# Four chunks on one token block instead of two chunks on two blocks: a fast-multiplication MLP on one core

## The chip, the core and the metric

The kernel runs on one core of a Trainium2 chip. The engines named here are PE (TensorE, matrix products into PSUM), DVE (VectorE), ACT (ScalarE), POOL (GpSimd) and SP (SyncE, whose queue issues nearly all DMAs). The metric is the device time of one execution in microseconds; the runs shown are compared by their median. All arithmetic is float32 at the interface. Inside, a float32 operand is split into a rounded part ("hi", type float32r) and the remainder ("lo"), and a product is made of three passes: hi x hi, hi x lo and lo x hi.

## What is computed

A transformer block with adaptive layer norm over S = 2048 tokens of width D = 576, with an MLP of hidden width F = 4608. Cut to what matters:

```python
mod = (silu(c) @ w_mod).reshape(c.shape[0], 6, 1, -1)
sa, ca, ga, sb, cb, gb = (mod[:, i] for i in range(6))
h = layernorm(x) * (1 + ca) + sa
x = x + ga * linear_attention(h, A_wqkv, A_wo)      # 32 heads of 18, phi(t) = where(t>0, t+1, exp(t)) + 1e-6
h = layernorm(x) * (1 + cb) + sb
x = x + gb * (silu(h @ B_w1) @ B_w2)                # 576 -> 4608 -> 576
```

## The kernel before

Tokens are handled in 16 tiles of 128 and 4 blocks of 512. The hidden width is handled in 18 groups of 256 (two chunks of 128, `G2 = 2`, `NG = 18`). The work has three stages.

**Stage A** (to about 213 us of the profiled span): the modulation, the projections to k, v and part of q, and the sums over tokens of the linear attention. The change leaves it as it is, except that the temporary `e` of `phi` (L348) is handed in by the caller.

**Stage B** (213 to 398 us): the loop `while s < NT + 5 or filler or turns` (L798). Step s normalises the attention numerator of tile s, transposes tile s-1 and projects tile s-2 (`attn_out`, L572). Once the four tiles of a block are done, the block is normalised again and "turned" (`turn_all`, L702): transposed to the layout [feature, token], modulated, split to hi and lo, and the sums of its pieces that the fast multiplication needs are formed, split and stored to DRAM (`store_h`, L683). The first MLP group (g = 0) is done in this stage plainly: `load_mlp(0)` (L582) loads and splits its weights, and `mlp_units` (L659) puts six pieces of work a block on a list called `filler`: two `mlp_up` (14 matmuls of 512 columns each) and four `mlp_down` (12 matmuls of 288 columns each). `unit()` takes the next piece off the list, `turn_chunk()` the next piece of a turn. The order of the instructions on each engine in this stage is chosen by the framework's planner from the program's order and its own estimate of the times.

**Stage C** (398 us to the end) does the other 17 groups by a fast multiplication with seven products in place of eight (Strassen-Winograd). A unit is one group and one pair of blocks (`units`, L1106), so 34 units. In the up direction the 2x2 split is over the two blocks of the pair, the two 256-wide halves of the first 512 features, and the two chunks of the group; the last 64 features come in two additional matmuls in four of the seven products. One up product (`passes`, L949) is 6 or 8 matmuls of 128x128 weights on 512 tokens. `Unit.up(n)` (L970) then gathers products in three PSUM banks: product 1 is copied out, product 2 is added to 1, and 6, 5, 7, 4, 3 are read by DVE between accumulations into the same bank, so that the four results f (two blocks by two chunks) appear, to which ACT applies SiLU. Order of products: (1, 6, 2, 5, 7, 3, 4).

In the down direction the split is over two halves of 256 tokens of one block, the two chunks, and the two halves of the 576 output columns; each block of the pair has its own seven products (`down`, L1040), each of 12 / 2 = 6 matmuls of 288 columns, followed by one DVE addition of the PSUM bank into `acc` or `U` (L1054). `operands1` and `operands2` (L1015, L1023) form the token-side sums on POOL and split them (cast on ACT, difference on DVE or POOL). Within a unit, PE's order is written by hand: two down products of the unit before stand around each up product.

```python
if before:
    before.down(2 * q)
unit.up(n)
if before:
    before.down(2 * q + 1)
```

Of the 14 up operands of the two pairs, 10 are streamed from DRAM for each group (`STREAM`, L679; `fetch`, L933) into three rooms, and 4 stay in SBUF. `Weights` (L866) loads a group's weights (w1 and w2), forms their seven sums on POOL and splits each (cast on ACT, difference on DVE, `sub_hi`, L61); w1 is prepared during the unit before the group's first, w2 during the group's first. Only PE has a hand-written order in this stage (`manual_schedule(engines={PE})`, L1093); the others follow the planner. The last block of the last group goes down plainly (`plain_down`, L1079), with each tile stored as it is done.

## Time and profile before

Three runs took 1216.33, 1218.12 and 1222.57 us, with a median of 1218.12. The profiled execution took 1217.73 us.

| what | value |
|---|---|
| time of the profiled execution | 1217.73 us |
| its span, first to last instruction | 1215.7 us |
| first up product of stage C starts | 397.84 us |
| last up product of stage C, its last matmul starts | about 1194.7 us |
| PE busy over the span | 1158.4 us, 95% |
| DVE busy over the span | 984.3 us, 81% |
| POOL, ACT busy over the span | 599.8 us, 518.2 us |
| granted TensorE clock, mean | 0.993 |
| HBM read, written | 250.56 MB, 16.78 MB |

How to read it: the span is the time from the first to the last instruction that the profiler recorded. An engine's busy time is the union of its instructions. Matmuls overlap in PE's pipeline, so one matmul's listed duration is longer than the step to the next one, and a busy PE need not be a PE at its highest rate. In a group of instructions, the line of the source, the engine, the operation and the tiles (result, then inputs) come first, then the count; behind the bar stand the busy time in us and the mean duration of one in ns, then the idle time of the engine ahead of them with what ended it. In a list of waits, the numbers are the total in us, how often, and the longest. In a timeline a row has the start in us, the time to the end of the row's last instruction, and how many were merged; an idle time ahead of it stands in brackets. In rows by stretch, each engine has its busy time and, in brackets, its number of instructions; the last columns are the granted clock, the DMA engines' mean busy share and GB/s. In the view of one line, the three numbers behind the count are the shortest, the median and the longest duration in ns.

### The profile page before, as it was taken

The page shows a single profiled execution, that of the slowest core. Times are in us where ns is not written, and L with a number is a line of the kernel's source. Part 1 is how long each engine was busy: PE and PEld are TensorE (multiplying, and loading weights), DVE is VectorE, ACT ScalarE, POOL GpSimd, SP SyncE. Part 2 cuts the span into 40 slices and gives each one's busy share as a digit, 9 for nine tenths or more (in the row PEclk, how much of TensorE's full clock was granted, in tenths as well). Part 3 has the DMA queues.
Part 4 walks back from the last instruction along what each step waited for, and adds up shares of the span by engine and source line. Part 5 has one row for each costly group of instructions (what it writes and reads, how often), then busy time and mean ns, then how long its engine had stood idle before and what let it go on. Part 6 is the DMA issues. An engine that isn't in the chain of part 4 may idle for free. (4 is left out here: it accounts for less than half of the span.)

```text
span 1215.7 us, 19355 instructions
## 1 busy us (share of the span) xinstructions
PE 1158.4 (95%) x7167; PEld 1048.1 (86%) x7167; DVE 984.3 (81%) x1591; ACT 518.2 (43%) x1057; POOL 599.8 (49%) x676
## 2 busy tenths in 40 slices
PE   5999999999998799999999999999999999999997
PEld 4999999899988688888888889888888888888896
DVE  6746754888866688888898898888888888888887
ACT  4434342315545444444444444444444444444441
POOL 3200000332400665775676577577657747766772
PEclk9999999999998999999999999999999999999999
DMA  9213300213247778868769779769678687697664
GB/s 289 82 40 88 113 1 1 70 41 128 101 181 286 277 250 297 308 239 326 271 248 340 257 252 336 260 247 340 247 283 310 235 333 272 243 344 260 242 253 147
DMA packets 57580, 268.60 MB, mean 221 GB/s; under 512 B 5450, under 2 KB 20046, under 8 KB 34446
## 3 DMA queue, kind: packets, MB, share of 16 engines
q1 hardware_dynamic: 57486, 267.36, 61.2%
q8 instruction: 57, 0.93, 0.3%
q14 instruction: 37, 0.30, 0.1%
HBM read 250.56 MB, written 16.78 MB: 220 GB/s over the span
## 5 line engine op out<-in xcount | busy, mean ns | idle before, releaser
L1054 DVE TENSOR_TENSOR acc<-down,acc 128x576 f32<-128x576 f32 x335 | 245.7, 748 | 22.2 <-PE down L1050 17.1
L962 PE MATMUL up<-hT,w 128*128 128x512 f32 x876 | 225.9, 393 | 2.1 <-DMA hT<-hd 2.1
L962 PEld LDWEIGHTS up<-hT,w 128*128 128x128 f32 x876 | 156.2, 188 | 28.2 <-DMA hT<-hd 1.6
L1026 POOL TENSOR_TENSOR s<-f,f 128x256 f32<-128x256 f32 x67 | 52.7, 786 | 251.1 <-ACT f L1001 251.1
L1050 PEld LDWEIGHTS down<-w,hb 128*128 128x128 f32 x804 | 112.7, 188 | 35.2 <-DVE U L1054 11.5
L1050 PE MATMUL down<-w,hb 128*128 128x288 f32 x804 | 127.2, 300 | 15.0 <-DVE U L1054 13.6
L1054 DVE TENSOR_TENSOR U<-down,U 128x576 f32<-128x576 f32 x134 | 100.7, 752 | 48.6 <-PE down L1050 47.6
L154 PE MATMUL psK<-w,hT 128*128 128x288 f32 (+2 forms) x896 | 127.8, 301 | 2.5 <-DVE e L129 1.1
L154 PEld LDWEIGHTS psK<-w,hT 128*128 128x128 f32 x896 | 122.7, 192 | 4.4 <-DVE hT L62 2.1
L1050 PE MATMUL down<-w,hc 128*128 128x288 f32 x804 | 122.7, 295 | 0.3 <-DVE acc L1054 0.2
L1050 PEld LDWEIGHTS down<-w,hc 128*128 128x128 f32 x804 | 115.4, 188 | 7.0 <-DVE acc L1054 1.4
L1011 POOL TENSOR_TENSOR hc<-s,hc 128x512 fp32r<-128x512 f32 x67 | 94.4, 1409 | 12.0 <-ACT hc L1010 12.0
L1010 ACT CAST hc<-s 128x512 fp32r<-128x512 f32 x67 | 41.6, 621 | 117.1 <-POOL s L1028 117.0
L62 DVE TENSOR_TENSOR w<-raw,w 128x288 fp32r<-128x288 f32 (+2 forms) x139 | 83.3, 609 | 7.4 <-ACT w L903 7.0
L1001 ACT ACTIVATE f<-f 128x512 f32<-128x512 f32 x102 | 64.3, 630 | 55.1 <-DVE f L1000 55.1
L962 PE MATMUL up<-room,w 128*128 128x512 f32 x330 | 85.6, 394 | 1.3 <-DVE f L986 0.9
L1050 PE MATMUL down<-w,hd 128*128 128x288 f32 x402 | 65.2, 297 | 5.0 <-DVE acc L1054 5.0
L962 PEld LDWEIGHTS up<-room,w 128*128 128x128 f32 x330 | 58.8, 188 | 11.5 <-DVE f L986 1.4
L1050 PEld LDWEIGHTS down<-w,hd 128*128 128x128 f32 x402 | 57.5, 188 | 11.4 <-ACT f L1001 6.3
L154 PE MATMUL big<-w,qT 128*128 128x288 f32 x448 | 65.8, 300 | 0.8 <-DVE qT L62 0.7
L1028 POOL TENSOR_TENSOR s<-s,f 128x256 f32<-128x256 f32 x67 | 64.6, 964 | 2.7
L962 PE MATMUL up<-hT,wt 128*128 128x512 f32 x206 | 64.9, 396 | 0.0
(228 smaller groups left out, 2367.5 us busy)
## 6 DMA issues: line engine op xcount, KB each, us to landing
hT<-hd SPq DMA_DIRECT2D x69, 1280.0 KB, 5.5
hT<-hd SPq DMA_DIRECT2D x43, 1024.0 KB, 5.7
room<-hd SPq DMA_DIRECT2D x32, 1280.0 KB, 5.8
room<-hd SPq DMA_DIRECT2D x23, 1024.0 KB, 5.7
raw<-in_B_w_dram SPq DMA_DIRECT2D x18, 576.0 KB
raw<-in_B_w_dram SPq DMA_DIRECT2D x18, 512.0 KB, 6.8
hd<-S SPq DMA_DIRECT2D x6, 1024.0 KB
xt<-in_A_x_dram SPq DMA_DIRECT2D x16, 288.0 KB, 4.0
```

The source lines that it names most:

```text
L62: return V.tensor_sub(lo, full, f32(hi))
L154: T.matmul(ps, xpart(a), wpart(b), start=n == 0, stop=n == len(XW) - 1)
L962: T.matmul(ps, left, right, start=first and m == 0, stop=m == len(seq) - 1, skip_group_check=True)
L1001: A.activation(f, f, AF.Silu)
L1010: A.copy(t[:, :, 0, :], src)
L1011: eng.tensor_sub(t[:, :, 1, :], src, f32(t[:, :, 0, :]))
L1026: G.tensor_add(s[:, 0:1], half(i, 0, 1), half(i, 1, 1))
L1028: G.tensor_sub(s[:, 1:2], s[:, 0:1], half(i, 0, 0))
L1050: T.matmul(ps[:, p, :HALF], self.a[i, n][:, u, p * P : (p + 1) * P], self.w.w2[n][:, v], start=n in (1, 5, 7, 6) and j == 0, stop=j == 2, ...
L1054: V.tensor_add(dst, ps[:, :, :HALF], dst)
```

## The change

Groups 0 and 1 are both done plainly in stage B; the other 16 groups are taken two at a time ("double groups" d = 1 to 8, 512 hidden features, four chunks). A unit of stage C is now one double group and one block of 512 tokens: 8 x 4 = 32 units. In the up direction the token split is over the block's two halves of 256 tokens (`HT`), and each of the seven products is made twice, for the two subgroups s = 0 and 1, side by side in one PSUM bank. So an up product is 12 or 16 matmuls of 256 columns. In the down direction each product accumulates both subgroups in one bank: 12 matmuls of 288 columns and then one DVE addition. There are seven down products a unit and PE's order has one behind each up product. The order of products becomes (1, 6, 2, 5, 7, 4, 3).

All seven up operands of every block go to DRAM and are streamed back for each unit into four rooms; none stays in SBUF. `turn_all` forms them for each block by itself, with the sums always on POOL, in the two `sl` buffers that the plain MLP's SiLU and the late q projections use as well. The raw weights of the plain groups pass through the one `hs` buffer. Up to step 7 one piece of filler work is taken a step, from step 8 on two.

The diff, cut to its core:

```diff
-    def load_mlp(g):
+    def load_mlp(g, pool, wt):
         f0 = g * FW
-        r1 = rawp.tile([P, KC + 1, FW], F32, name="raw")
+        r1 = new_hs((P, KC + 1, FW), F32)
...
-        r2 = rawp.tile([P, KC + 1, FW], F32, name="raw").rearrange("p k f -> p (k f)")[:, : G2 * D]
+        r2 = new_hs((P, G2, D), F32)
...
-    ORDER = (1, 6, 2, 5, 7, 3, 4)
+    ORDER = (1, 6, 2, 5, 7, 4, 3)
...
+        S = [wqp.tile([P, 4, 2 * HT], F32R, name="S", bufs=2) for _ in range(2)]
+        for c in range(2):
+            t0, t2 = temp(), temp()
+            turn_chunk_k(tb, c, t0)
+            turn_chunk_k(tb, 2 + c, t2)
+            (a11, a21), (a12, a22) = ((t[:, :HT], t[:, HT:]) for t in (t0, t2))
+            G.tensor_sub(a11, a11, a21)
+            G.tensor_add(a21, a21, a22)
+            split_s(S[0], c, t0)
+            G.tensor_sub(a22, a22, a11)
+            G.tensor_sub(a12, a12, a22)
+            split_s(S[1], c, t2)
+            yield
+        t = temp()
+        turn_chunk_k(tb, KC, t)
+        for w in ws:
+            up, down = mlp_units(tb, w)
             filler.extend(up + down)
...
         if s == 4:
-            w = load_mlp(0)
+            ws = [load_mlp(g, pool, M[2][:, 1 + g, :512].rearrange("p (a f) -> p a f", a=2))
+                  for g, pool in enumerate((wg, wg2))]
...
-        unit()
+        unit(1 if s < 8 else 2)
...
-    for p in (px, rawp, pc, wp, wg, h2p):
+    for p in (pb, px, wg2, pc, wp, wg, hTa, wqp):
         p.release()
...
+    pools = [tc.alloc_tile_pool(name=n, bufs=1, reuse_waits="tile") for n in ("w1", "w2", "pf", "ph", "wm", "rm")]
+    rooms = [rm.tile([P, 5, HT], F32R, name=f"room{i}") for i in range(4)]
+    ND = (NG - 2) // 2
...
         def up(self, n):
-            w = self.w1[n] = w1p.tile([P, 4, P], F32R, name="w1", bufs=8)
-            A.copy(w[:, 0:2], self.b1[n])
-            sub_hi(w[:, 2:4], self.b1[n], w[:, 0:2])
+            w = self.w1[n] = w1p.tile([P, 2, 4, P], F32R, name="w1", bufs=8)
+            for s in range(2):
+                b = self.b1[s][n]
+                A.copy(w[:, s, 0:2], b)
+                sub_hi(w[:, s, 2:4], b, w[:, s, 0:2])
...
+            h, w, wt = rooms[used % 4], self.w.w1[n], self.w.wt
+            for s in range(2):
+                seq = [(w[:, s, b], h[:, a, :]) for c in range(2) for a, b in ((c, c), (c, 2 + c), (2 + c, c))]
+                if k is not None:
+                    f = s * FW + k * P
+                    seq += [(wt[:, i, f : f + P], h[:, 4, :]) for i in range(2)]
+                for m, (left, right) in enumerate(seq):
+                    T.matmul(ps[:, s], left, right, start=first and s == 0 and m == 0, stop=m == len(seq) - 1,
+                             skip_group_check=True)
+            fetch(used + 4)
+            used += 1
...
+        def operands(self, n):
+            f = self.f
+            if n == 2:
+                self.split(1, f[0, 0], V)
+            elif n == 7:
+                self.split(4, f[1, 1], V)
+            elif n == 4:
+                s1, s2 = (pf.tile([P, 2, HT], F32, name=n) for n in ("s1", "s2"))
+                G.tensor_add(s1, f[1, 0], f[1, 1])
+                G.tensor_sub(f[1, 0], f[0, 0], f[1, 0])
+                self.split(7, f[1, 0], G)
+                G.tensor_sub(s2, s1, f[0, 0])
+                self.split(5, s1, G)
+                self.split(6, s2, G)
+                self.s2 = s2
+            elif n == 3:
+                self.split(2, f[0, 1], V)
+                G.tensor_sub(f[0, 1], f[0, 1], self.s2)
+                self.split(3, f[0, 1], G)
...
             for p in range(2):
-                for j, (u, v) in enumerate(((0, 0), (0, 1), (1, 0))):
-                    T.matmul(ps[:, p, :HALF], self.a[i, n][:, u, p * P : (p + 1) * P], self.w.w2[n][:, v],
-                             start=n in (1, 5, 7, 6) and j == 0, stop=j == 2, skip_group_check=True)
+                tok = slice(p * P, (p + 1) * P)
+                for j, (s, a, b) in enumerate((s, a, b) for s in range(2) for a, b in ((0, 0), (0, 1), (1, 0))):
+                    T.matmul(ps[:, p, :HALF], self.a[n][:, a, s, tok], self.w.w2[n][:, s, b],
+                             start=n in (1, 5, 7, 6) and j == 0, stop=j == 5, skip_group_check=True)
...
-        units = [(g, p) for g in range(1, NG) for p in range(2)]
+    units = [(d, b) for d in range(1, ND + 1) for b in range(NB)]
...
             for q, n in enumerate(ORDER):
-                if before:
-                    before.down(2 * q)
                 unit.up(n)
                 if before:
-                    before.down(2 * q + 1)
...
+                    before.down(q)
+                if final:
+                    unit.plain_operands(n)
+                else:
+                    unit.operands(n)
+                if b == 0:
+                    ws[d].down(Unit.DOWN[q])
+                if b == NB - 1 and d < ND:
+                    ws[d + 1].up(n)
```

More of the change, by code (lines that the diff above doesn't have):

```diff
@@ L784 @@
+        for n, at in ((3, 0), (6, HT)):
+            store_h(tb, n, S[1][:, :, at : at + HT])
+        yield
     turns, filler = [], []
@@ L961, in passes @@
-            for m, (left, right) in enumerate(seq):
-                T.matmul(ps, left, right, start=first and m == 0, stop=m == len(seq) - 1, skip_group_check=True)
-            if i is not None and i >= 3:
-                fetch(i + 3)
+            nonlocal used
+            h, w, wt = rooms[used % 4], self.w.w1[n], self.w.wt
+            for s in range(2):
+                seq = [(w[:, s, b], h[:, a, :]) for c in range(2) for a, b in ((c, c), (c, 2 + c), (2 + c, c))]
[5 more added lines that the diff above has]
+                             skip_group_check=True)
@@ L1104 @@
         ws = {1: w}
-        ph, before = None, None
-        units = [(g, p) for g in range(1, NG) for p in range(2)]
-        for g, p in units:
-            unit = Unit(g, p, ws[g])
-            more = g + 1 < NG
-            if p == 1 and more:
-                ws[g + 1] = Weights(g + 1)
-                ws[g + 1].load1()
-                ws[g + 1].sums1()
+        before = None
+        for m, (d, b) in enumerate(units):
+            unit = Unit(m, ws[d])
+            final = m + 1 == len(units)
+            if b == NB - 1 and d < ND:
+                w = ws[d + 1] = Weights(d + 1)
+                for f in (w.load1, w.sums1):
+                    for s in range(2):
+                        f(s)
+            if b == 0:
+                for s in range(2):
+                    ws[d].sums2(s)
@@ L1146 @@
+            if b == NB - 1 and d < ND:
+                for s in range(2):
+                    ws[d + 1].load2(s)
+            before = unit
+        for t in (2, 3, 0, 1):
+            unit.plain_down(t)
     psC.release()
-    for p in (rs, ph, pf, wm, w1p, w2p, wqp, hTa, accp):
+    for p in pools[::-1] + [accp]:
         p.release()
```

358 lines of the change are left out of this document (118 added, 240 removed).

## The prediction

> **What bounds the kernel now.** First the page's busy shares, then the busy times by stage.
>
> ```profile
> PE 1158.4 (95%) x7167; PEld 1048.1 (86%) x7167; DVE 984.3 (81%) x1591; ACT 518.2 (43%) x1057; POOL 599.8 (49%) x676
> ```
>
> ```profile
> core 0: us, PE busy (x) PEld busy (x) DVE busy (x) ACT busy (x) POOL busy (x), PEclk, DMA share, GB/s
> 213.00:397.80 184.80, 171.88 (x1154) 160.90 (x1152) 149.34 (x267) 80.04 (x130) 48.05 (x38) 0.97 0.38 134
> 397.80:1194.80 797.00, 775.02 (x4466) 680.80 (x4467) 690.47 (x1059) 348.89 (x758) 521.91 (x605) 1.00 0.76 278
> 1194.80:1215.70 20.90, 14.39 (x98) 12.94 (x96) 14.93 (x20) 2.28 (x4) 4.18 (x4) 1.00 0.44 157
> ```
>
> The first 213.0 us (stage A) are not touched. The rows are stage B (attention output and the plain MLP group), stage C (34 units of seven products) and the tail. PE is never far from full, so I price it by the step from one matmul's start to the next, from the timeline:
>
> ```profile
> 78.44 1.22 PE L390 MATMUL kvp<-pk,vx 128*128 128x256 f32 x9
> 79.50 0.70 PE L154 MATMUL psK<-w,hT 128*128 128x288 f32 x4
> ...
> 717.84 1.75 PE L1050 MATMUL down<-w,hc 128*128 128x288 f32 x12
> 719.42 1.55 PE L962 MATMUL up<-hT,w 128*128 128x512 f32 x6
> 720.82 0.40 PE L962 MATMUL up<-hT,wt 128*128 128x512 f32 x1
> ```
>
> Twelve matmuls of 288 columns take 1.58 us (132 ns each), six of 512 1.40 (232), nine of 256 1.06 (118; another nine 1.08, so I take 119). Stage C: 34 units of 50 up matmuls are 1700 x 0.232 = 394.4, 33 units of 84 down matmuls (the 34th lie in the tail) 2772 x 0.1317 = 365.1, sum 759.5: 37.5 of the 797.0 us are PE standing. Stage B by the same steps: 448 + 168 + 192 matmuls of 288 columns (106.4), 112 of 512 (26.0), 160 transposes at 109 ns (17.4), some 10 for the fp32 products before them: 159.6, so 25.2 standing. What PE stands for, from the waits in 420 to 1190 us and the end of stage B:
>
> ```profile
> PE down L1050 <- DVE U L1054: 13.1, 26, 1.5
> PE down L1050 <- DVE acc L1054: 3.4, 4, 1.2
> ```
>
> ```profile
> 379.76 2.88 PE L641 MATMUL small<-hT,w 128*128 128x512 f32 x12
> 385.04 1.05 PE L655 MATMUL big<-w,hs 128*128 128x288 f32 x6 [2.40 <-ACT hs L644]
> 386.80 8.61 PE L655 MATMUL big<-w,hs 128*128 128x288 f32 x42 [0.70 <-DVE hs L62]
> ```
>
> In stage C it is one kind: a down product waits until VectorE has emptied its bank (16.5 us). VectorE is 87% busy there (690.5 of 797.0), and these are its groups:
>
> ```profile
> L1054 DVE TENSOR_TENSOR acc<-down,acc 128x576 f32<-128x576 f32 x335 | 245.7, 748 | 22.2 <-PE down L1050 17.1
> L1054 DVE TENSOR_TENSOR U<-down,U 128x576 f32<-128x576 f32 x134 | 100.7, 752 | 48.6 <-PE down L1050 47.6
> L1000 DVE TENSOR_TENSOR f<-up,f 128x512 f32<-128x512 f32 x68 | 46.6, 685 | 5.4 <-PE up L962 4.7
> L914 DVE TENSOR_TENSOR raw<-raw,bc_gb 128x576 f32<-128x576 f32 x34 | 33.4, 1023 | 3.2 <-DMA raw<-in_B_w_dram 3.2
> ```
>
> **The change, part by part.**
>
> *Up matmuls.* 32 units of 100 matmuls of 256 columns: 3200 x 0.119 = 380.8 us. Two cost 238 ns where one of 512 cost 232: 0.3 us a unit, 9.6 in all, all on the path. Bounds: 117.8 and 120 ns, 377 to 384 us. [...]
>
> *Down matmuls.* 84 a unit still, since two chunk pairs accumulate in one bank: 31 x 84 x 0.1317 = 342.9. With the ups 723.7, against 759.5 for two units more.
>
> *Group 1 done plainly.* Four blocks of 28 matmuls of 512 columns and 48 of 288: 4 x (28 x 0.232 + 48 x 0.1317) = 51.3 us added to stage B, where PE is the scarce engine. VectorE gets 16 more evacuations (0.755 each, 12.1) and 8 hs splits (0.68, 5.4), beside PE. Its weights need four loads on SP (two of 64 rows, 512 and 576 KB) and four VectorE steps like those of group 0 (1.21, 0.41, 1.29 and 2.08: 5.0 us) at a time, 232 to 290 us, when VectorE has no gap: half of it shows, +2.5 (0 to 5). All four large raw loads now pass one after the other through the `hs` buffer; group 0's pair took from 227 to 251, so two pairs end near 275, before the first `hs` is written (294). If they end later, the x rows queued behind them on SP are late.
>
> *Standing in stage B.* 25.2, plus 2.5; the waits of 2.0 and 0.9 us near 331 to 338 are filled by the doubled filler work; the last block still ends with the 2.4 and 0.7 above, but the 2.4 us that stage C's first matmul waited for its weights go: their raw tiles now lie where attention's tiles were (free at 360), and the four last plain downs (6.3 us) cover the first splits (two of 0.41 on ACT, two of 0.6 on VectorE). 22 us; bounds 14 (only the switch from stage A stays) and 38 (a rival).
>
> *Evacuations in stage C.* 7 a unit for 14: 217 against 469 (and four plain ones in both), 252 x 0.749 = 189 us of VectorE gone. A bank's next product comes after another product and two ups, 4.4 us or more, where it could be one product and one up. So the 16.5 us of waits go. VectorE per four units (4 x 23.0 us): 28 x 0.75 + 20 x 0.685 + 12 splits x 0.73 + w1 (14 x 0.6 + 2 x 0.86) + gb (4 x 1.02) + w2 (14 x 0.6) = 66 of 92, 72%. But the w2 work falls into the first unit of four and w1's into the last: there it is near full.
>
> *Operand sums on POOL.* 8 operations of 512 columns at 1.3 to 1.4 us (L1011 hc: 1.41) for 14 shorter ones: 11 of 23 us. Product 7's operand, the most urgent, is f after up 4 (0.2 + 0.69 + 0.63), two or three sums (2.6 to 3.9), cast and difference (2.0): 6 to 8 us after up 4; PE comes to it after 9.4. Hidden; were POOL 2 us late, every unit would wait.
>
> *Streams.* Every product's operand comes from DRAM, where now 4 of 14 stay in SBUF: 4.2 MB a unit, some 180 GB/s against 278 now. Four rooms, so a fetch has three products and downs, 9.8 us; 1280 KB landed in 5.5. Hidden. More stores in stage B (ten of at most 640 KB a block, in 1 KB pieces), on SP behind x rows that are wanted far later; the last block's have some 38 us of plain units before stage C reads.
>
> *Order 7, 4, 3.* Product 4 adds to the bank that VectorE reads after product 7, with one down (1.58) between. After 7 VectorE's add ended 0.9 us after the next down began (718.04 + 0.69 against 717.84). So 0.7 us are spare; in the 16 weight-laden units I take 0.2 us each (3.2), 0 to 1.0 as bounds.
>
> *Standing in stage C.* 37.5 is some 8 at the start, 16.5 of waits, 13 in bits. After: start 6 (the first unit has no downs to cover 7 to 4, and w2 comes as late as now), bits 12, 3 for the order: 21; bounds 12 and 45.
>
> *Tail.* 20.9 now. After: 4 x 24 plain matmuls 12.6, one wait 0.5, and 3.8 from the last matmul to the end as now: 16.9.
>
> **Sum.** 213.0 + (159.6 + 51.3 + 22) + (723.7 + 21) + 16.9 = 1207.5 us of span, against 1215.7. The profiled execution took 2.0 more than its span (1217.73), and the median of the runs is 0.4 above that: 1209.5, so **1210** as a median, 0.7% faster. 0.5% (6 us) is about what this kernel can tell from no change.
>
> **Rivals.**
>
> *Stage B stretches.* Each block's turn now holds both `sl` buffers through its sums; in block 1 that took from 311 to 331 us, and no up ran then (PE had attention to do). For blocks 2 and 3, with fewer attention tiles left, 5 to 8 us of standing each: 1222. Against it: POOL's sums are half as long there, and downs remain. Decides from 8 us on.
>
> *VectorE late at product 4 (slower).* VectorE's SBUF-only steps already take longer when POOL runs:
>
> ```profile
> L1011 DVE TENSOR_TENSOR ha<-f,ha x33: 413/656/1026, 424.9 to 803.2; 128x256 fp32r<-128x256 f32 x33
> L1011 POOL TENSOR_TENSOR hc<-s,hc x33: 1286/1307/1804, 439.1 to 815.9; 128x512 fp32r<-128x512 f32 x33
> ```
>
> With POOL's steps twice as long, one ahead of the add can be held 1.3 us, past the 0.7 spare: 0.7 us in each of 31 units, 22 us, 1232. From 0.26 us a unit the gain is gone. Against it: the adds read PSUM and their own times are even (682 to 686 ns). [...]
>
> *More gain.* Stage B's gaps filled (16) and stage C clean (12): 1195.
>
> **Numbers.** Forecast (1200 to 1219) 0.42, stage B 0.22, product 4 0.24, more gain 0.12. Faster (below 1212): 0.29 + 0.03 + 0 + 0.12 = 0.44; same: 0.13 + 0.14 + 0.04 = 0.31; slower: 0.05 + 0.20 = 0.25. The range 1194 to 1234 leaves out half of the last case and a third of the slow one's, 0.14.
>
> **What would show it.** Some 8810 matmuls; up steps of 119 ns; VectorE near 70% in stage C; the waits on L1054's evacuations gone; stage B some 232 us; the stretch from the first up matmul to the end some 762. Wrong if PE waits for VectorE before product 4, for POOL before product 7, or stands over 30 us in stage B.

## The result, and the profile after

The changed kernel takes 1254.35 us as a median (1249.34 to 1259.97), against 1217.22 us of the kernel before on the same chip: a ratio of 1.030, 95% interval 1.024 to 1.035. It is slower, and outside the predicted range of 1194 to 1234. The profiled execution is the shortest of its four, 1249.34 us with a span of 1247.6.

The page's busy shares of the changed kernel, then its busy times by stage (stage B, stage C, tail; the columns are those of the rows shown before):

```profile
PE 1176.7 (94%) x8809; PEld 1150.5 (92%) x8809; DVE 841.8 (67%) x1309; ACT 490.4 (39%) x944; POOL 551.3 (44%) x471
```

```profile
210.40:459.70 249.30, 225.32 (x1455) 207.83 (x1453) 179.86 (x326) 103.37 (x183) 77.28 (x78) 0.97 0.36 117
459.70:1230.70 771.00, 743.07 (x5804) 737.38 (x5805) 528.79 (x732) 298.30 (x594) 448.17 (x363) 0.99 0.60 198
1230.70:1247.60 16.90, 12.90 (x98) 12.67 (x96) 5.18 (x8) 1.25 (x2) 0.00 (x0) 1.00 0.32 118
```

DVE lost 142 us of work, as the change means it to, and fell to 69% of stage C. The span is 31.9 us longer all the same. Stage A ends 2.6 us earlier, stage B takes 64.5 us more, stage C 26.0 less and the tail 4.0 less. "Standing" is, here and below, a stage's time less its matmuls at their undisturbed steps. In stage B the matmuls account for 51.3 of the 64.5 us (group 1), and standing for 13.2. In stage C the matmuls are 32.6 us fewer, but standing rose from 37.5 to 44.1, where the prediction let it fall to 21.

What PE waits for in the changed kernel, over the whole span (total, times, longest):

```profile
PE down L999 <- DVE U L1002: 14.0, 7, 2.1
PE up L911 <- DVE f L929: 7.6, 7, 1.9
...
PE small L641 <- ACT sl L127: 5.4, 4, 1.8
PE small L142 <- ACT sl L127: 4.2, 1, 4.2
PE big L655 <- ACT hs L644: 3.9, 1, 3.9
...
PE up L911 <- DVE acc L657: 3.3, 1, 3.3
PE down L999 <- DVE acc L1002: 3.1, 7, 0.4
PE up L911 <- DVE f L950: 2.7, 1, 2.7
PE big L655 <- DVE acc L657: 2.3, 1, 2.3
```

The wait for U was 13.6 us in the kernel before, over 27 times; it is 14.0 now, over seven. Seven is the number of double groups after the first, and a place that comes once in a double group is once in four units. The four units of one double group in the changed kernel, each from its first up matmul to that of the next unit, then the first unit of the double group ahead of it, and 50 us of the kernel before, by stretch (first PE, PEld, DVE, ACT, POOL busy, then clock and DMA):

```profile
645.40:673.20 27.80, 23.94 (x187) 23.33 (x186) 24.70 (x33) 11.43 (x26) 19.45 (x17) 1.00 0.53 185
673.20:697.10 23.90, 23.32 (x185) 23.09 (x185) 14.13 (x20) 8.99 (x18) 17.84 (x17) 1.00 0.72 231
697.10:720.20 23.10, 23.10 (x186) 23.10 (x185) 11.19 (x15) 7.11 (x13) 10.57 (x9) 1.00 0.56 183
720.20:743.30 23.10, 23.10 (x186) 23.10 (x185) 17.35 (x27) 11.19 (x25) 10.96 (x9) 1.00 0.60 196
...
547.60:575.30 27.70, 25.20 (x186) 24.75 (x186) 24.60 (x33) 11.26 (x25) 19.36 (x17) 0.94 0.55 181
```

```profile
450.00:475.00 25.00, 25.00 (x148) 22.52 (x147) 21.09 (x34) 11.63 (x28) 16.89 (x21) 1.00 0.96 357
475.00:500.00 25.00, 24.03 (x139) 20.80 (x138) 22.04 (x34) 9.74 (x21) 16.72 (x20) 1.00 0.63 215
```

Before, DVE was busy 84% and 88% in these two stretches. Now it is 89, 59, 48 and 75% in the four units. All PE's idle time lies in the first (3.9 us) and in the second (0.6). The whole preparation of w2, for two groups at once, falls into that first unit. The other double groups repeat this: counted from up matmul to up matmul and less the undisturbed steps, the first units of the seven later double groups stand 4.6 to 5.1 us each (33.0 together), their second units 3.8 together, the first two units of the stage 6.5, and all the others 0.6 together. In three of the seven first units the granted clock is 0.94 and in four 1.00, and all but the last are equally long (27.7 us): PE's speed does not set their length. PE's rows with a wait there, and DVE's queue at the same time (start, time, and the idle time ahead in brackets):

```profile
650.50 1.82 PE L999 MATMUL down<-w,h 128*128 128x288 f32 x12 [0.43 <-DVE acc L1002]
...
656.32 1.88 PE L999 MATMUL down<-w,h 128*128 128x288 f32 x12 [2.10 <-DVE U L1002]
...
663.03 1.69 PE L911 MATMUL up<-room,w 128*128 128x256 f32 x12 [1.33 <-DVE f L929]
```

```profile
647.71 1.97 DVE L864 TENSOR_TENSOR raw<-raw,bc_gb 128x576 f32<-128x576 f32 x2 [2.97 <-DMA raw<-in_B_w_dram]
649.60 0.75 DVE L1002 TENSOR_TENSOR acc<-down,acc 128x576 f32<-128x576 f32 x1
650.27 0.83 DVE L958 TENSOR_TENSOR h<-f,h 128x512 fp32r<-128x512 f32 x1
651.02 3.61 DVE L864 TENSOR_TENSOR raw<-raw,bc_gb 128x576 f32<-128x576 f32 x2
654.56 1.04 DVE L62 TENSOR_TENSOR w<-raw,w 128x288 fp32r<-128x288 f32 x1
655.52 0.74 DVE L1002 TENSOR_TENSOR U<-down,U 128x576 f32<-128x576 f32 x1
```

DVE stands 2.97 us for the load of w2 (its raw buffers were held until w1's splits were done). Then the multiplications by gb stand ahead of the addition into U that PE waits for, and two of them take 3.61 us. From 647.71 us on DVE's timeline lists no idle time until 669.1. This reading has two possible causes, the amount of work in the unit or its order at the head, and the experiments had to tell them apart.

### The profile page after: what moved, and what is told of

Its sections match the earlier page's. It is cut to its first block, busy times and chain, and to the rows that moved or that the text cites. A ratio compares the mean times of both kernels' runs of the same rounds, so it can differ in the third digit from the quotient of the medians.

```text
span 1247.6 us, 21904 instructions
## 1 busy us (share of the span) xinstructions
PE 1176.7 (94%) x8809; PEld 1150.5 (92%) x8809; DVE 841.8 (67%) x1309; ACT 490.4 (39%) x944; POOL 551.3 (44%) x471
## 4 chain that ended last, share of the span: by engine, by line
PE 70%; DVE 15%; DMA 8%; POOL 2%; ACT 2%; issue 2%; SPq 1%; DVEq 0%; ACTq 0%; POOLq 0%
PE up L911 23%; PE down L999 21%; PE psK L154 12%; DMA raw<-in_B_w_dram 6%; PE small L641 4%; DVE w L62 4%; PE big L655 3%; PE big L154 3%; DVE raw L864 3%; PE kvp L389 1%; DVE acc L1002 1%; PE down L1034 1%; DVE h L958 1%; DMA acc<-in_A_wqkv_dram 1%; DVE f L950 1%
## 5 line engine op out<-in xcount | busy, mean ns | idle before, releaser
L999 PE MATMUL down<-w,h 128*128 128x288 f32 x2604 | 384.4, 296 | 17.4 <-DVE U L1002 14.0
L911 PE MATMUL up<-room,w 128*128 128x256 f32 x2688 | 384.9, 286 | 13.8 <-DVE f L929 7.6
L999 PEld LDWEIGHTS down<-w,h 128*128 128x128 f32 x2604 | 357.0, 190 | 20.4 <-DVE U L1002 15.4
L911 PEld LDWEIGHTS up<-room,w 128*128 128x128 f32 x2688 | 353.5, 194 | 16.7 <-DVE f L929 9.4
L1002 DVE TENSOR_TENSOR acc<-down,acc 128x576 f32<-128x576 f32 x155 | 116.5, 752 | 59.3 <-PE down L999 58.6
L951 ACT ACTIVATE f<-f 128x512 f32<-128x512 f32 x96 | 60.7, 633 | 197.0 <-DVE f L950 197.0
L957 ACT CAST h<-f 128x512 fp32r<-128x512 f32 x159 | 95.3, 616 | 52.6 <-POOL f L978 47.7
L911 PE MATMUL up<-room,wt 128*128 128x256 f32 x512 | 104.2, 285 | 0.0
L958 POOL TENSOR_TENSOR h<-f,h 128x512 fp32r<-128x512 f32 x62 | 92.6, 1494 | 12.6 <-ACT h L957 12.6
L958 DVE TENSOR_TENSOR h<-f,h 128x512 fp32r<-128x512 f32 x97 | 80.7, 832 | 16.3 <-ACT h L957 15.1
L62 DVE TENSOR_TENSOR w<-raw,w 128x288 fp32r<-128x288 f32 (+1 forms) x130 | 84.6, 683 | 8.4 <-ACT w L852 8.1
L958 POOL TENSOR_TENSOR h<-s,h 128x512 fp32r<-128x512 f32 x62 | 87.2, 1407 | 0.7 <-ACT h L957 0.7
L950 DVE TENSOR_TENSOR f<-up,f 128x512 f32<-128x512 f32 x64 | 44.0, 688 | 41.5 <-PE up L911 41.4
L62 DVE TENSOR_TENSOR w<-t,w 128x256 fp32r<-128x256 f32 (+1 forms) x96 | 64.1, 696 | 2.5 <-ACT w L852 2.1
```

Of the source, the lines that this page charges most:

```text
L62: return V.tensor_sub(lo, full, f32(hi))
L911: T.matmul(ps[:, s], left, right, start=first and s == 0 and m == 0, stop=m == len(seq) - 1, skip_group_check=True)
L950: V.tensor_add(f, ps, more)
L951: A.activation(f, f, AF.Silu)
L957: A.copy(t[:, 0], src)
L958: eng.tensor_sub(t[:, 1], src, f32(t[:, 0]))
```

## The experiments

All times are medians of several executions, and ratios are to the kernel before on the same chip (1217 to 1220 us). The run without group 1 was executed once. Stage B is counted from the first matmul of L501 to the first up matmul, and is 245.6 us with 39.2 standing in the changed kernel; stage C is counted from its first to its last up matmul, and is 769.4 us with 44.0 standing.

| run | edit to the changed kernel | median us | ratio (95%) | stage B | stage C | standing in C |
|---|---|---|---|---|---|---|
| (change) | none | 1254.35 | 1.030 (1.024 to 1.035) | 245.6 | 769.4 | 44.0 |
| e1 | w2's preparation held back | 1269.42 | 1.041 (1.038 to 1.044) | 239.4 | 788.9 | 63.5 |
| e2 | three temporaries sl | 1246.24 | 1.024 (1.020 to 1.027) | 237.8 | 770.8 | 45.4 |
| e3 | group 1 left out | 1228.36 | one execution | 212.6 | 779.8 | 54.4 |
| e4 | order 7, 3, 4 | 1392.86 | 1.143 (1.140 to 1.147) | 245.5 | 910.3 | 184.9 |
| e5 | no multiplication by gb | 1226.76 | 1.008 (1.006 to 1.011) | 244.4 | 747.3 | 22.0 |
| e6 | that on POOL | 1266.81 | 1.040 (1.038 to 1.043) | 242.8 | 787.4 | 62.1 |
| e7 | three sl, w1's first splits later | 1247.36 | 1.025 (1.023 to 1.027) | 229.5 | 780.0 | 54.6 |
| e8 | three raw buffers, three rooms | 1241.26 | 1.020 (1.017 to 1.022) | 243.7 | 760.7 | 35.3 |
| e9 | w2's differences on DVE | 1256.13 | 1.032 (1.030 to 1.035) | 243.2 | 777.5 | 52.2 |
| e10 | w1's differences too | 1266.48 | 1.040 (1.037 to 1.042) | 244.0 | 781.1 | 55.7 |
| e11 | e2, e8 and e9 together | 1233.68 | 1.013 (1.011 to 1.016) | 239.8 | 758.4 | 33.1 |
| e12 | w2's last splits in the second unit | 1281.24 | 1.050 (1.047 to 1.053) | 246.2 | 797.6 | 72.3 |
| e13 | e2, e8 and e12 together | 1236.01 | 1.013 (1.010 to 1.017) | 239.9 | 756.9 | 31.6 |
| e14 | addition into U ahead | 1245.22 | 1.022 (1.020 to 1.024) | 244.5 | 766.2 | 40.8 |
| e15 | e2, e8 and e14 together | 1255.38 | 1.031 (1.028 to 1.033) | 241.8 | 776.4 | 51.0 |
| e16 | six steps more, first unit | 1292.93 | 1.061 (1.058 to 1.063) | 244.5 | 808.0 | 82.5 |
| e17 | six steps more, third unit | 1255.07 | 1.030 (1.027 to 1.032) | 244.6 | 774.9 | 49.5 |

Stage spans are of one profiled execution each. The one of the changed kernel lies 5 us below its median, so a difference of a few us in a stage means little. Stage A, whose work is the same in all these runs, ends anywhere from 213 to 222 us, so that medians and stages need not move by the same amount.

### Is it the order on VectorE's queue? (e1)

```diff
-            if b == 0:
-                for s in range(2):
-                    ws[d].sums2(s)
...
-                    before.down(q)
+                    plain[0] = before.down(q)       # down() returns its DVE addition
...
-                    ws[d].down(Unit.DOWN[q])
+                    with behind([plain[0]]):
+                        if q in (1, 2):
+                            ws[d].sums2(q - 1)
+                        for p in {3: (1, 7), 4: (2, 4), 5: (5, 6), 6: (3,)}.get(q, ()):
+                            ws[d].down(p)
```

> Edit: in the first unit of each double group the preparation of w2 (the four multiplications by gb, the splits) is queued on VectorE behind the additions of the down products: the first two multiplications behind the one of place 1, the other two behind place 2, the splits behind places 3 to 6. Same work, same unit, other order; product order and stage B unchanged. Theory A (head of the queue): in the changed kernel VectorE stood with a multiplication at the head of its queue until the raw rows landed (21.6 us in 7 waits), and two more took 3.6 us ahead of an evacuation, so PE waited about 5.6 us once per double group (7 times 39 us) for the banks. Then stage C falls from 771 to about 740 us, the waits for U and acc from 17 to under 5 us, and the time from 1254 to about 1224. Theory B (load): the first unit of four simply has too much VectorE and POOL work, whatever its order: stage C stays above 763 and the time above 1245.

Measured: 1269 us, 15 us more than the change. The theory that held the order alone to be at fault gave 1224 and falls, in this form of the order at least. The waits of the run with the preparation held back:

```profile
PE up L913 <- DVE f L952: 31.0, 14, 4.5
...
PE up L913 <- DVE f L931: 4.5, 6, 1.4
```

No wait for U is left. In its place PE waits 31.0 us, 14 times, for the read of an up bank between products 7 and 4 (L952 here is L950 of the changed kernel). That is the wait of the prediction's slower rival, and it comes from the preparation's work, now later.

### Stage B: the two temporaries, and group 1 (e2, e3, e7)

```diff
-        phi(ps, acc[t], pool.tile([P, D], F32, name=name, bufs=2))
+        phi(ps, acc[t], pool.tile([P, D], F32, name=name, bufs=2 if pool is pa else 3))
...
-        t = pc.tile([P, D], F32, name="sl", bufs=2)
+        t = pc.tile([P, D], F32, name="sl", bufs=3)
```

> Edit: three sl buffers in place of two, nothing else. Theory C: the turn of a block holds both sl buffers through its POOL sums, so the next two transposes, SiLU and the late q projections wait; PE stood 4.2 and three times 1.1 to 1.2 us in the turn of block 0 (284 to 296 us) and 1.8 and 1.3 us in that of block 3, and the granted clock was 0.67 from 292 to 304 us. With a third buffer stage B falls from 249 to about 240 us and the time to about 1245. Rival: the chain through POOL and ACT sets it, not the buffers: under 3 us.

> Edit: the plain MLP work of group 1 is left out of stage B (its weights are still loaded and split); the output lacks group 1's share. My sum: group 1 costs PE 51.3 us, and stage B loses more than that only if group 1 also brings waits: 249 falls to 198 us if the matmuls alone are its price, to under 190 if it brought a good part of the standing, and above 203 if a part of its matmuls filled gaps. Stage C unchanged at 771.

The third buffer takes 8 us off the time and 7.8 off stage B, and leaves stage C as it was. PE in the turn of block 0, changed kernel, then two stretches by the columns as above (the clock is the third from the end), then the second stretch with three buffers:

```profile
289.60 1.11 PE L142 MATMUL small<-ident,xn 128*128 128x128 f32 x4 [4.17 <-ACT sl L127]
291.84 2.92 PE L641 MATMUL small<-hT,w 128*128 128x512 f32 x6 [1.13 <-ACT sl L127]
295.96 4.33 PE L641 MATMUL small<-hT,w 128*128 128x512 f32 x10 [1.19 <-ACT sl L127]
```

```profile
289.60:299.80 10.20, 7.88 (x19) 5.60 (x20) 5.00 (x7) 5.99 (x10) 4.18 (x5) 0.50 0.55 185
292.00:304.00 12.00, 10.81 (x34) 8.19 (x35) 4.40 (x6) 6.80 (x11) 3.78 (x5) 0.67 0.83 277
```

```profile
292.00:304.00 12.00, 12.00 (x50) 9.38 (x50) 6.24 (x8) 8.30 (x13) 3.59 (x4) 0.88 0.66 220
```

A turn holds both buffers through its sums; the next transposes and the SiLU of the plain group must wait for one. The granted clock is 0.50 in the 10.2 us behind the stand of 4.17. Over 292 to 304 us it is 0.67, and 0.88 with the third buffer: 34 matmuls against 50 in the same time.

Without group 1 (`for w in ws[:1]` in place of `for w in ws`) stage B is 33 us shorter, not 51.3: its standing rises from 39.2 to 57.5. So 18 of group 1's 51 us come back as standing without it. Part of that can be slow matmuls and not idle time: the granted clock is 0.972 over the span of this run, against 0.985 in the changed kernel.

The third edit keeps the three buffers and holds w1's first splits behind the last split of hs (`with behind(plain[1]): w.up(n)`).

> Two edits in stage B: three temporaries sl in place of two, and the splits of w1 for the first double group are queued behind the last split of hs of the plain groups. Stage C's code is unchanged. If the 9 to 10 us of standing at stage B's end (3.9 before the last plain downs, 2.3 and 3.3 at the start of stage C) come from the preparation put ahead of them: some 5 us less than the 1246 of three temporaries alone, about 1241. If the preparation then is late for the first ups: no gain, 1246 or more.

The time stays that of e2. Stage B is another 8 us shorter, but stage C's first unit pays it back with a wait of 6.0 us for L951 (L950 of the changed kernel). At the start of stage C both w1 and w2 of the first double group are prepared at once; put back, the work is late at another place.

### The order of the products (e4)

```diff
-    ORDER = (1, 6, 2, 5, 7, 4, 3)
+    ORDER = (1, 6, 2, 5, 7, 3, 4)
```

(The sums in `operands` move with it.)

> Edit: product order 7, 3, 4 in place of 7, 4, 3 (the sums with s2 move behind product 4), nothing else. My slow rival in the prediction (VectorE late at product 4) would have it that the time falls by some 20 us. Theory A: PE waited only 2.7 us there, once, in the first unit; so stage C gets 1 to 4 us shorter, and the plain end some 2 us longer, because product 4's operand is the last: within 5 us of 1254.

Missed by far: 1393 us. The waits of that run:

```profile
PE down L998 <- POOL h L958: 66.2, 31, 3.0
PE down L998 <- ACT h L957: 55.7, 15, 7.3
```

In this kernel the order 7, 4, 3 does not cost its predicted 3.2 us, it saves 139 against 7, 3, 4: product 4's result is the source of product 7's operand, and POOL's chain to it has no time if 4 comes last.

### How much of it is the multiplication by gb? (e5, e6)

> Left out: the multiplications of w2 by gb in stage C (28 steps of 128x576 on VectorE), so the output lacks that factor for groups 2 to 15; matmuls and everything else stay. Theory load (in the first unit of four VectorE has more to do than the 24 us allow; the multiplications take 5.6 us of it at 1.4 us each): TensorE's 5.6 us of standing per double group fall to about 1, so stage C is some 30 us shorter (771 to about 741) and the time about 1224. Theory wait (VectorE stands 3.0 us for the second operand's load with evacuations queued behind; the load and not the steps is what is late): the splits wait for the load in place of the multiplications, stage C is only some 10 us shorter, the time about 1244.

> Only the engine of the multiplications by gb in stage C changes: POOL in place of VectorE. Theory load (VectorE alone is too full in the first unit): VectorE's 5.6 us go, evacuations come in time, stage C is 15 us or more shorter, the time 1240 or less. Rival (VectorE and POOL are both near full in that unit, POOL busy 18.5 of 24 us, and POOL makes the operands of product 7): TensorE waits for POOL's h before product 7, stage C is as long as before or longer, the time 1254 or more.

(There are 32 such steps, in groups 2 to 17; the text on record counted 28 and 15.) Without the steps the time is 27.6 us less and standing in stage C halves, to 22.0; the theory of the load (of work) expected 1224 and is met at 1227. No wait for U is left in it, but this run takes away both the steps and what they block. On POOL the time is 12 us more, as the rival said: PE then waits 17.6 us for POOL's h and 19.6 for f (L929).

Why four multiplications cost 5.6 us is in the view of their line, beside that of the additions that read PSUM (shortest, median, longest in ns), in the changed kernel:

```profile
L864 DVE TENSOR_TENSOR raw<-raw,bc_gb x32: 744/1352/1851, 449.5 to 1140.2; 128x576 f32<-128x576 f32 x32
...
L1002 DVE TENSOR_TENSOR acc<-down,acc x155: 740/757/758, 484.5 to 1230.9; 128x576 f32<-128x576 f32 x155
```

Laid beside POOL's rows, the 9 multiplications with POOL idle take 744 to 758 ns, and the 13 with POOL busy throughout 1836 to 1848. The additions take 757 ns with POOL idle and 751 with POOL busy (medians). A split of the weights (L62) is 419 ns alone and 1042 beside POOL (medians over stage C, beside POOL for at least half of the step, where it ranges from 409 to 1550; the text on record for e9 has 940).

### Earlier load, and differences on another engine (e8, e9, e10, e11)

```diff
-    rooms = [rm.tile([P, 5, HT], F32R, name=f"room{i}") for i in range(4)]
+    rooms = [rm.tile([P, 5, HT], F32R, name=f"room{i}") for i in range(3)]
...
-            t = wm.tile([P, KC + 1, FW], F32, name="raw", bufs=2)
+            t = wm.tile([P, KC + 1, FW], F32, name="raw", bufs=3)
...
                 for f in (w.load1, w.sums1):
                     for s in range(2):
                         f(s)
+                w.load2(0)
...
-                for s in range(2):
-                    ws[d + 1].load2(s)
+                ws[d + 1].load2(1)
```

> One edit in stage C: three raw buffers in place of two (and three rooms for the operands in place of four, to make space), so that the load of the first half of w2 is issued at the start of the fourth unit and not at its end. Theory wait (the load is late and VectorE stands 3.0 us for it): the standing in the first unit falls from 5.6 to under 3 us per double group, stage C is about 20 us shorter, the time about 1235. Theory load (what matters is the work in that unit): the half that moves into the fourth unit gives part of this, 5 to 15 us. If three rooms are too few, TensorE waits for the rooms' loads, which the trace shows separately.

13 us less by the medians, 8.7 in stage C, where standing is 35.3: within the 5 to 15 that the load theory allows, and short of the 20 that the wait theory asked for. The wait for U falls from 14.0 to 8.6, but a wait for POOL's h (7.5 us, seven times, the longest 1.1) is new. PE waits for a room once, 0.5 us, so three are enough.

```diff
-            self.b2[s] = self.winograd(*parts, [t[:, i] for i in range(3)])
+            self.b2[s] = self.winograd(*parts, [t[:, i] for i in range(3)], V)   # its four differences on DVE
```

> Only the engine of w2's differences in stage C changes: VectorE in place of POOL (8 steps of 128x288 per double group). In the changed kernel a multiplication by gb takes 747 ns where POOL is idle and 1845 ns where POOL works all along, a split of w2 419 against 940 ns. Theory shared access (VectorE is slowed by POOL's steps next to it, more than by the count of its own steps): the 8 added steps cost some 3.4 us (0.42 each), the multiplications fall to about 750 ns (2.6 us less per double group) and the splits by some 3 us, so VectorE has about 2 us less to do in the first unit, TensorE's standing falls from 5.6 us to 3 or less, and the time by 15 to 25 us, to about 1234. Theory count (what matters is how many steps VectorE has): 3.4 us more per double group, the time 1265 or more.

> As the run before, and w1's differences too are VectorE's (another 8 steps of 128x256 per double group, in the fourth unit). Shared access: the splits of w1 shorten as well (719 towards 400 ns), so nothing is lost in the fourth unit, and the time is that of the run before or up to 8 us less. Count: the fourth unit, where VectorE is busy 17.9 of 24.5 us, takes 3 us more and stays clear of standing, but the first unit starts later: the run before plus 5 us or more.

Neither theory's number came: 1256, no change. The multiplications still average 1409 ns (1406 in the changed kernel); POOL, rid of the differences, still has its operand sums to do. PE's waits move from U (14.0 to 4.1) to the other down banks (11.5) and the up banks (14.3). With w1's differences on DVE too it is 12 us slower than the change and 10 slower than e9, which is what the theory of the count asked for. To move this work away from POOL did not end the slowing.

> w2's differences on VectorE, three raw buffers with three rooms, three temporaries sl: the gains of the single runs (8 us from sl, 13 from raw, and 15 to 25 from the differences) do not add, since the last two work on the same 5.6 us per double group. Shared access: standing in stage C near the 22 us without the multiplications, stage B 8 us shorter, the time about 1222. Count: about 1240. The kernel before (1218) is not expected to be beaten: the tensor work of the changed kernel, counted in undisturbed steps, is some 20 us more in stages B and C.

1233.7 us, the shortest version found that leaves nothing out, and between the two expectations. That is e2 and e8 added up (8 and 13 us), with nothing from e9. It still does not reach the kernel before.

### Amount or order? (e12 to e17)

```diff
-                    before.down(q)
+                    added = before.down(q)          # down() returns its DVE addition
...
-                if b == 0:
+                if b == 0 and q < 4:
                     ws[d].down(Unit.DOWN[q])
+                if b == 1 and q < 3:
+                    with behind([added]):
+                        ws[d].down(Unit.DOWN[4 + q])
```

> One edit in stage C: of the seven splits of w2 per double group, the last three by place (5, 6, 3) are made in the first three slots of the second unit and not in the first unit; all of w2's loads, multiplications and differences stay where they are. Theory peak (the two groups' w2 lies in one unit of 24 us; what counts is VectorE's work in that unit): 6 of the 14 split steps, some 4.5 us at 0.75 each, leave the first unit for the second, where VectorE has 7 us to spare, and the standing per double group falls from 5.6 us to about 2, as it did without the multiplications: stage C some 25 us shorter, the time about 1230. Theory start (the multiplications and the 3.0 us for their load stand ahead of the evacuations and are what is late, whatever follows them): the standing stays above 4.5 us and the time above 1247.

27 us slower, and the wait for U stays at 14.0, 7 times. By the numbers it is the theory of the start. But the run has a side effect that decides it. The waits of PE, then those of POOL in 480 to 1200 us:

```profile
PE down L999 <- POOL h L958: 23.3, 8, 3.7
PE down L999 <- DVE U L1002: 14.0, 7, 2.1
```

```profile
POOL t L829 <- DMA raw<-in_B_w_dram: 54.5, 6, 10.3
```

The raw tiles are now held into the second unit, the next w1 is loaded later, and POOL, which waits for nothing of the kind in the changed kernel, stands for it with its operand sums queued behind. So this run does not tell the theories apart.

> The run before, with three raw buffers and three rooms, and three temporaries sl. Peak: another 8 us in stage B and up to 10 in stage C, the time 1215 to 1222, level with the kernel before. Start: the raw buffers alone help, as in the combined run, the time about 1233.

With the third raw buffer POOL's wait for the load falls to 22.5 us and the time is 1236. The gains of e2 and e8 alone would add up to 1233, so nothing is added by the spreading; no run has those two edits and nothing else.

```diff
-            if b == 0:
-                for s in range(2):
-                    ws[d].sums2(s)
...
-                if before:
-                    before.down(q)
+                added = before and before.down(q)
...
+                if b == 0 and q == 0:
+                    with behind([added] if before else []):
+                        for s in range(2):
+                            ws[d].sums2(s)
```

> One edit in stage C: w2's multiplications by gb are queued on VectorE behind the addition of the first place's down bank (U), and so are no longer ahead of it; the splits stay with the planner. In the changed kernel TensorE waits for that addition 14.0 us in all, 2.1 in each first unit, and 7.6 us for later reads of up banks. Theory start (the head of the first unit blocks the addition while VectorE waits for the load): the 14.0 us go, the 7.6 stay or grow to at most 12, the time 1240 to 1248. Theory peak (the same work in the same unit): the wait moves to the up banks or to the next down banks, the standing per double group stays within 1 us of 5.6 and the time within 6 us of 1254.

> The run before, with three raw buffers and three rooms, and three temporaries sl. Start: with the first half's load early and the addition ahead, stage C stands some 20 to 25 us, the time 1217 to 1226. Peak: no more than the combined run gave, 1230 to 1236.

The waits of e14:

```profile
PE up L911 <- DVE f L950: 14.5, 8, 2.9
PE up L911 <- DVE f L929: 9.1, 11, 1.4
```

The 14.0 us for U are gone, and the waits for the up banks grew from 10.3 to 23.6. The time is 9 us less by the medians, but stage C only 3.2, so the order at the head is worth a small part; the larger part only moves. Put together with the buffers it is no gain at all (1255). The trace of e15 shows why the early load is lost there: two splits of w1 (2.2 us) have slipped into the first unit, ahead of the addition into U, and all four multiplications are held behind them. They begin 6.9 us into that unit, against 3.9 in e14 and 2.3 in the changed kernel. PE then waits 16.5 us for L950 and 7.7 for L929.

The last pair adds work that nothing uses, at one place or the other:

```diff
-                if before:
-                    before.down(q)
+                added = before and before.down(q)
+                if b == 0 and q == 0 and before:          # e17: b == 2
+                    with behind([added]):
+                        for _ in range(6):
+                            V.tensor_mul(more, bc["gb"], bc["gb"])
```

> Added and used by nothing: six multiplications of 128x576 on VectorE in the first unit of each double group but the first (42 in all, 747 ns each alone, so 4.5 us a unit), queued behind the addition of the first place. Theory peak (the first unit has no room left on VectorE): TensorE stands most of that longer, 3 to 5 us per double group, 20 to 35 us in all, the time 1274 to 1290. Theory start (only what stands ahead of the first addition hurts; behind it there is room): under 1 us per double group, the time 1254 to 1261.

> The same six multiplications in the third unit of each double group (48 in all), where VectorE is busy 12.0 of 24.5 us. Peak: nothing is late there, the time 1252 to 1258. If VectorE's whole amount of work set the time (69% of stage C is its share), this run would be as long as the one before.

The added steps of both runs (shortest, median, longest), and the waits of PE that grew, of the run with the first unit and then of the run with the third:

```profile
L1073 DVE TENSOR_TENSOR more<-bc_gb x42: 739/742/1354, 562.3 to 1196.1; 128x576 f32<-128x576 f32 x42
...
PE up L912 <- DVE f L930: 25.1, 7, 4.5
...
PE down L1000 <- POOL h L959: 7.5, 7, 1.7
```

```profile
L1073 DVE TENSOR_TENSOR more<-bc_gb x48: 747/969/1732, 510.0 to 1205.5; 128x576 f32<-128x576 f32 x48
...
PE up L912 <- DVE f L930: 11.4, 9, 1.9
```

In the first unit, behind the addition into U, 42 steps cost 38.6 us, 5.5 us per double group for 5.1 us of busy time. In the third unit 48 steps, which are even longer there (6.6 us of busy time), cost 0.7 us, which the spread of the runs covers, and none of the nine waits for L930 lies in a third unit. So it is the amount of DVE work in the first unit that sets its length, nearly one for one, and neither its head alone nor DVE's share of the stage.

## Why the prediction was wrong, by its own steps

- **Matmuls.** 8809, as said. The up step measured 120 ns against 119, at the upper bound: 384.0 us for 380.8, 3.2 us. The down step is 132.5 ns in undisturbed units against 131.7, 2 us over the stage, which the sums here leave in the standing. The stages were summed rightly (with the 2.0 and 0.4 us the median comes to 1209.9 and not 1209.5, which leaves the 1210), and the tail's 16.9 us were met.
- **Stage A** ended 2.6 us early, within the 9 us by which its end differs between the executions here.
- **Standing in stage B** was put at 22 us (14 to 38) and is 38.4. The rival "Stage B stretches" named the mechanism (a turn holds both sl buffers), and e2 shows a price of 8 us; it was placed in blocks 2 and 3, and the largest wait is in block 0, where the forecast saw none. The other half is at the end. The 2.4 us of stage C's first matmul were to go, since the splits have room early; instead the planner put w1's splits ahead of the last hs, and the multiplications by gb, with a wait for their load, ahead of the plain downs' additions (3.9, 2.3 and 3.3 us). In the one other order that was tried (e7) it comes back in the first unit.
- **Evacuations in stage C.** Half as many (217) as said, and DVE lost 142 us of work in all; "so the 16.5 us of waits go" is the step that failed. They were read as a matter of count and of distance between products, by the average load. The prediction itself says that the first unit is "near full", and then prices nothing but a start of 6 us for it. By its own terms that unit holds 7 x 0.75 + 5 x 0.685 + 3 x 0.73 + 4 x 1.02 + 14 x 0.6 = 23.3 us of DVE work in 23.0 us. Measured, the same 33 steps are 24.7 us, and PE stands 33.0 us in the first units of the seven later double groups and 3.8 in the second ones; with the 6.5 at the start that is nearly all of the 44.1, where 21 were forecast. What failed is a sum over four units where one unit sets the time; e16 and e17 show it. The sum itself was good: 67.4 us of DVE work in four units for the 66 forecast. The term for gb at 1.02 us a step, taken from the kernel before, was also short: 1.4 here.
- **Order 7, 4, 3.** Its price of 3.2 us did not show: in the changed kernel one wait of 2.7 us at that place, in the first unit of the stage. The rival "VectorE late at product 4" gave 1232 by 0.7 us in each unit. In the changed kernel that wait came only this once, and e1 and e9 show it as soon as the work is moved there (31.0 and 14.3 us). Its mechanism, POOL stretching the step ahead of an addition, is one that acts, at other places: before the third down product (two multiplications of 1.84 and 1.85 us beside POOL, and PE waits 2.10 us in the unit at 645.4 us) and before product 7 (a split of 1.55 us, and PE waits 1.33). That a step can be held 1.3 us was the author's estimate from POOL's 1307 ns; the longest stretch of a multiplication by gb measured in the changed kernel is 1.1 us (744 to 1851 ns).
- **Operand sums on POOL, streams.** Hidden, as said: no wait of that kind is among the listed ones of the changed kernel. They come when an edit takes POOL's slack (66.2 us in e4, 17.6 in e6, 23.3 in e12, 7.5 in e8).
- **Net.** The forecast was a gain of 8.2 us of span out of 11.5 us more tensor work and 19.7 us less standing. The tensor work came out at 14.7 more, standing at 19.8 more, and stage A at 2.6 less: 31.9. Of the signs of being wrong, "PE stands over 30 us in stage B" is the one that came true plainly. Of the times given in the rivals none reached 1254: each was priced alone, and here the one for stage B came together with waits in stage C that no rival had at their place.

What stays open: how the 44 us of stage C divide between order, load and amount. By stage C, e14 puts the order at the head at 3 us, e8 the earlier load at 9 (9 and 13 by the medians), and e5 the multiplications with all that they block at 22. No run mends the order and keeps the gain of the earlier load, since e15 lost the one with the other. Nor does any of these runs account for the first two units of the stage (6.5 us).

## What to carry to other kernels

If a change makes units shorter, work that comes once per group is packed into less time: add up the steps of the one unit where it falls, at the durations that they have there, and do not go by the stage's mean, which fell here from 87 to 69% while PE waited more. A wait that is mended by order alone is likely to appear at the next reader of the same engine (in e14 14.0 us went at U and 13.3 came at the up banks); to test for that, add idle work at the full place and at the empty one. And where PE stands anyway, as beside attention here, work added there is paid only in part (33 of 51 us in e3).

## What the runs showed of the hardware

In the changed kernel a VectorE multiplication of 128x576 with both inputs in SBUF is 747 ns with POOL idle and 1844 with POOL at work throughout, and an addition of the same size that reads PSUM is 757 and 751 (medians). POOL's steps are stretched too: the two beside the slow pair at 651 to 655 us are 512 columns wide and take 1.74 and 1.81 us, against 1.30 for the same step (L958) at 645.85 us. Which of the two is longer differs: in the kernel before, 13 multiplications by gb took 746 to 748 ns beside a POOL step of 256 columns (L1028), and there it was POOL's step that took 1.36 to 1.37 us, against 0.73 for the shortest of that line.

PE's granted clock was 0.50 in the 10.2 us behind a stand of 4.17 us, and steps of 512 columns (L641) were 427 ns there, against 227 at full clock (medians). The clock also fell behind shorter stands: to 0.50 for 3.4 us behind one of 2.06 us in the first unit at 547.6 us, and in two more of the seven, while in the other four it stayed at 1.00, behind stands of 2.10 us among them. So these runs give no length of stand from which on the clock falls.

```profile
558.45 2.60 PE L999 MATMUL down<-w,h 128*128 128x288 f32 x12 [2.06 <-DVE U L1002]
```

```profile
559.20:562.60 3.40, 3.40 (x18) 3.40 (x17) 3.40 (x5) 0.17 (x1) 3.40 (x4) 0.50 0.15 61
```

So a stand can cost more than itself, as in block 0, where the steps of 512 columns behind it were 427 ns and not 227. In those first units it does not: the three with the lower clock take 27.7 us, as long as the ones at full clock.
